# Memory-augmented recurrent transformer: another split of a PSUM copy, dense weights in more pieces, and a reordered norm in step 2

## The chip, the cores and the metric

The kernel runs on one core of one Trainium2 chip. The metric is the device time of one execution in microseconds (us). A core has five engines that run side by side: TensorE (matrix multiply, writes its results to PSUM), VectorE, ScalarE and GpSimd (elementwise work), and SyncE, which here issues the DMAs. Each engine runs its own queue of instructions in order and waits on semaphores for the others. In the profile the engines are PE (TensorE's matmuls), PEld (its weight loads), DVE (VectorE), ACT (ScalarE), POOL (GpSimd) and SP (SyncE). "L567" is line 567 of the kernel.

## The reference

Two layers, applied twice. Layer A is attention over segments of 32 tokens, with 8 memory rows that are carried from segment to segment; layer B is a two-matrix feed-forward with ReLU. In short:

```python
# x [1, 2048, 512], 64 segments of 32 tokens; 32 heads of 128; 8 memory rows
def A(x):
    mem = mem0
    for s in range(64):
        h = concat([mem, x[32*s : 32*s+32]])          # 40 rows
        q, k, v = h @ Wq, h @ Wk, h @ Wv              # 32 heads x 128
        p = softmax(mask(q @ k.T * 128**-0.5))        # 40 x 40 a head
        o = (p @ v) @ Wo                              # 40 x 512
        mem, out[s] = o[:8], o[8:]                    # memory for the next segment
def B(x): return relu(x @ w1) @ w2                    # 512 -> 1376 -> 512
x = x + A(layernorm(x)); x = x + B(layernorm(x))
x = x + A(layernorm(x)); x = x + B(layernorm(x))      # same weights
```

## The kernel before

**Steps.** The memory makes the 64 segments of a layer sequential. The kernel interleaves the two passes: step k handles segment k of the first pass (layer index 0) and segment k - 3 of the second (index 1), so that there are 67 steps, 0 to 66. Steps 0 to 2 and 64 to 66 have one pass only ("single"), steps 3 to 63 have both. The dense layer of a segment runs one step behind its attention.

**Order.** TensorE, VectorE, SyncE and GpSimd run in the order in which `step` writes their instructions (`tc.manual_schedule`); ScalarE's order is chosen by the framework's scheduler, with the blocks under `tc.high_priority` first.

**One step.** In `step(k)`:

- `qk(0, ..)` (L567) computes queries and keys of heads 0 to 15 in three batches. ScalarE copies the queries out of PSUM (L573, QT), VectorE the keys (L575, KT). `behind={n: f}` calls f after batch n.
- `load_values` and `load_memory_values` issue the DMAs that bring the values of the tokens and of the memory rows into `Vs`; `transpose_step` issues a transposing DMA that turns the normalized rows `XN` of the step before into `xnT`, input of the dense layer and of the second pass.
- `masks` (L593) writes the mask into a score bank, `scores` (L601) adds q times k to it, `exponentials` (L619 maximum, L623 subtract, L625 exponential on ScalarE) and `softmax` (L635 sum, L636 reciprocal, L639 multiply) make the probabilities.
- `probabilities` finishes the softmax of the first sixteen heads behind the first batch of the second `qk`, turns it by a transposing DMA (`turn_p`) and, in step 1, calls `load_dense`, which loads all dense weights (w1 1376 KB, w2 1280 and 96 KB). Until then w1's and w2's tiles serve as staging for values (`first_step`).
- `dense_h` (L510, hp) and `dense_y` (L526, into the second score bank sp) are the dense layer; `values1` (L373, v) makes the values of the second pass for the next step; `output_late` (wox) and `add_late` (L420) finish the second pass's output.
- `turn_second` turns the second sixteen heads' probabilities with TensorE (L655) into PSUM and copies them to `PT_sb` (L660). In steps with both passes there are four tiles: u = 0 and 1 (eight heads each), g = 0 and 1. The two of u = 0 lie in the pool `ps_c`, those of u = 1 in `ps_fill`.
- `weighted_v` (L692, pv) multiplies by the values into three tiles a pass: heads 0 to 11, 12 to 23 and 24 to 31. The second tiles take the `ps_c` banks of u = 0, the third ones the `ps_fill` banks of u = 1. `outputs` (L709) copies them to `OTm` and `OTx`.
- `output_mem` (L609, wo), `new_memory` (which starts `output_own`, L387), `make_room` (the rest of `output_own`) and `memory_values` (L767, vm) make the next memory and its values. `prepare` adds the residual and norms the step's rows (`moments` L260, `normalize_parts` L271 to L283, with GpSimd's power at L278).

**Step 2** is special: there the second pass starts. `first_later`, called behind the first `qk` batch of the second half, adds the dense layer of segment 0 (`add_dense`), norms the result for the second pass, writes it to the upper half of `XN` and turns it by DMA; `values1(3, ..)` reads the result before `dense_y`.

Of the kernel before, what the change touches and what calls it, by code (L numbers as in the profile page):

```python
# [22 lines left out]
def kernel(  # L23
# [14 lines left out]
    nc = tc.nc  # L38
    _, S, Dm = A_x.shape
# [3 lines left out]
    Dff = B_w1.shape[1]  # L43
# [26 lines left out]
    def has0(k):  # L70
        return 0 <= k < NSEG

    def has1(k):
        return DELTA <= k <= LAST
# [79 lines left out]
    w1_flat = w1_sb[:].rearrange("p c f -> p (c f)")  # L154
    w2_flat = w2_sb[:].rearrange("p c d -> p (c d)")

    def load_dense():
        nc.sync.dma_start(out=w1_sb[:], in_=B_w1.rearrange("(c p) f -> p c f", p=128))
        nc.sync.dma_start(out=w2_sb[:, 0:NFC - 1, :],
                          in_=B_w2[F_LAST:Dff, :].rearrange("(c p) d -> p c d", p=128))  # L160
        nc.sync.dma_start(out=w2_sb[0:F_LAST, NFC - 1, :], in_=B_w2[0:F_LAST, :])

    mhalf_t = const.tile([128, 2], F32)
# [94 lines left out]
    def moments(d, i):  # L258
        n = 64 if i else 64 * slots(d)
        nc.vector.bn_stats(out=stats_all[0:n, i, 0, :], in_=residual(d)[0:n, :])  # L260
# [2 lines left out]
        later = has1(k + 1) and k > 2  # L263
        return [(k - 1, 0)] + ([(k - 2, 1)] if later else [])

    def normalize_parts(parts):
        i0, i1 = parts[0][1], parts[-1][1] + 1
        for q in range(2 * max(slots(d) if i == 0 else 1 for d, i in parts)):
            o = q ^ 1
            j0, j1 = (i0, i1) if q < 2 else (0, 1)  # L270
            nc.vector.tensor_copy(out=stats_all[32 * q:32 * q + 32, j0:j1, 1, :],  # L271
                                  in_=stats_all[32 * o:32 * o + 32, j0:j1, 0, :])
        mv = wk.tile([128, 2, 3], F32, tag="ln_mv", bufs=2, name="mv")
        for _, i in parts:
            nc.vector.bn_aggr(out=mv[:, i, 0:2], in_=stats_all[:, i].rearrange("p n s -> p (n s)"))
        rstd = mv[:, i0:i1, 2]
        nc.vector.tensor_scalar_add(out=rstd, in0=mv[:, i0:i1, 1], scalar1=LN_EPS)
        nc.gpsimd.tensor_tensor(out=rstd, in0=rstd, in1=mhalf_t[:, 0:i1 - i0], op=ALU.pow)  # L278

        def rows():  # L280
            for d, i in parts:
                n = 64 if i else 64 * slots(d)
                nc.vector.tensor_scalar(out=XN[0:n, HALF * i:HALF * i + HALF], in0=residual(d)[0:n, :],  # L283
                                        scalar1=mv[0:n, i, 0:1], scalar2=mv[0:n, i, 2:3],
                                        op0=ALU.subtract, op1=ALU.mult)

        return rows
# [9 lines left out]
    def transpose_step(k):  # L297
        tag, bufs = ("R", 8) if k == 1 else ("xnT", 1)
        t = xnT_tiles[k] = wk.tile([128, NC4, 128], BF, tag=tag, bufs=bufs, name="xnT")
        n = 2 if k < 3 else NC4  # L300
        nc.sync.dma_start_transpose(out=t[:, 0:n, :], in_=XN[:, 0:128 * n])

    def first_later():

        add_dense(0)
        moments(0, 1)
        normalize_parts([(0, 1)])()
        nc.sync.dma_start_transpose(out=xnT_tiles[2][:, 2:4, :], in_=XN[:, HALF:Dm])

    def later_rows(k):  # L310
        return [xnT_tiles[k][:, 2 + c4 % 2, SEG * (c4 // 2):SEG * (c4 // 2) + SEG] for c4 in range(NC4)]
# [49 lines left out]
    def values1(s, ii, late=False):  # L361
        if not has1(s):
            return
        if ii == 0:
            vd1[s] = dram.tile([2, 4, 32, 512], BF, tag="vd1", bufs=3, name="vd1")
        values_tile(later_rows(s - 1), ii, vd1[s], late=late)
# [164 lines left out]
    def add_dense(d):  # L531
        n = 64 * slots(d)
        R = residual(d)
        if not has0(d):
            ob = obs[d] = wk.tile([128, HALF], BF, tag="ob", bufs=1, name="ob")
            nc.vector.tensor_tensor(out=ob[0:n, :], in0=R[0:n, :], in1=sp_banks[1][0:n, 0:HALF], op=ALU.add)
        else:
            nc.vector.tensor_tensor(out=R[0:n, :], in0=R[0:n, :], in1=sp_banks[1][0:n, 0:HALF], op=ALU.add)
            g, o = place1(d + DELTA)
            nc.gpsimd.tensor_copy(out=residual(g)[64 * o:64 * o + 64, :], in_=R[0:64, :])  # L540
# [40 lines left out]
    def qk(hf, act, between=None, behind=None):  # L581
        res = []
        for n, (o, nh) in enumerate(BATCHES):
            res.append((o, nh) + qk_batch(n, 16 * hf + o, nh, act[0], act[-1] + 1, None if n else between))
            if behind and n in behind:
                behind[n]()
            if hf and n > 0 and (n == 2 or len(act) == 1):
                masks(*act[n - 1:n])
        return res
# [38 lines left out]
    def softmax(hf, act, by_pe=False, ess=None):  # L628
        if ess is None:
            ess = exponentials(act)  # L630
        if by_pe and hf:
            transpose_p()
        for a, es in ess.items():
            sm = wk.tile([128, 8], F32, tag="sm", bufs=2)
            nc.vector.tensor_reduce(out=sm[:], in_=es[:], axis=AX.X, op=ALU.add)  # L635
            nc.vector.reciprocal(out=sm[:], in_=sm[:])  # L636
            eng = nc.vector if by_pe or (hf, a) == (1, act[-1]) else nc.gpsimd
            P = P1_sb if hf else P_sb
            eng.tensor_tensor(out=P[:, :, 64 * a:64 * a + L], in0=es[:],  # L639
                              in1=sm[:].unsqueeze(2).to_broadcast([128, 8, L]), op=ALU.mult)  # L640

    def turn_second(single=False):

        tps = {}
        for u in range(2):
            for g in range(2):
                if single and u:
                    tps[u, g] = tps[0, g][:, 4:8]
                    continue
                pool, tag = (ps_fill, "fill") if u else (ps_c, "c")  # L650
                tps[u, g] = pool.tile([128, 8 if single else 4, L], F32, tag=tag, name="tp")
            for sl in range(4):
                for g in range(2):
                    R = 64 * g
                    nc.tensor.matmul(tps[u, g][:, sl, :], lhsT=P1_sb[R:R + L, 4 * u + sl, :],  # L655
                                     rhs=ident[R:R + L, R:R + L], start=True, stop=True)
        ns = 8 if single else 4
        for s0 in range(0, 8, ns):
            for g, copy in ((0, nc.scalar.copy), (1, nc.vector.tensor_copy)):
                copy(out=PT_sb[:, s0:s0 + ns, g, :], in_=tps[s0 // 4, g][:, 0:ns])  # L660

    def transpose_p():
# [111 lines left out]
    def load_memory_values(k, act):  # L774
        for ii in range(2):
            for a in act:
                nc.sync.dma_start(out=Vs[64 * a:64 * a + M, 2048 * ii:2048 * (ii + 1)].rearrange("m (j e) -> m j e", j=4),
                            in_=vmds[k][ii, :, a * M:(a + 1) * M, :].rearrange("j t e -> t j e"))
# [82 lines left out]
    def make_room(k):  # L861
        if has0(k):
            output_own(k, H // 2, H)
        else:
            values1(k + 1, 1)
        output_ride(k)
# [49 lines left out]
    def step(k):  # L916
# [33 lines left out]
        value_group(k, 0, 0, 2)  # L950
        value_unit(k, 0)
        with tc.high_priority(offset=PRIO):
            transpose_step(k)
            load_memory_values(k, act)
            scores(qks, act)
            ess = exponentials(act)
            if not single:
                masks(act[0])
# [3 lines left out]
        def probabilities():  # L962

            softmax(0, act, by_pe, ess)
            if not by_pe:
                turn_p()
            if k % 4 == 3 and has_x:
                inputs_T(n_x)
            if has0(k + 1):
                load_x(k + 1)  # L970
            if k == 1:
                load_dense()

        def turn_first():
            probabilities()
            if k == 2:
                first_later()

        with tc.high_priority(offset=PRIO):
            qks = qk(1, act, behind={0: turn_first})  # L980
        if single:
            output_late(k, first, second)
        if k != LAST and not (single and has0(k)):
            dense_h(d)
        with tc.high_priority(offset=PRIO):
            scores(qks, act)
            softmax(1, act, by_pe)
        evict_behind.append(last_exp[0].ins)
        value_group(k, 0, 2, NC4, late=True)
        value_unit(k, 1)  # L990
# [4 lines left out]
        if k == LAST:  # L995
            dense_h(d, slice(0, 1))
        output_late(k, second, H)
        if has0(k) and has1(k + 1):
            values1(k + 1, 0)
        if not (single and has0(k)):  # L1000
            value_group(k, 1, late=True)
        value_group(k, 2, late=True)
        if has0(k) and has1(k + 1):
            values1(k + 1, 1, late=True)
        evict_behind.clear()
        if k == LAST:
# [9 lines left out]
            mom["x"] = stat_tail(mom["stats"])  # L1016
        with tc.high_priority(offset=PRIO):
            turn_second(single)
        tokens_in(k + 1)
        if k < LAST and spare_T(k + 1) is not None:  # L1020
            nc.gpsimd.tensor_copy(out=HTm[:, :, 2 * M:32], in_=spare_T(k + 1))
# [16 lines left out]
        if cont:  # L1038
            with tc.high_priority(offset=PRIO):
                new_memory(k, cont, wo)  # L1040
            make_room(k)
            with tc.high_priority(offset=PRIO):
                memory_values(k + 1)
        with tc.high_priority(offset=PRIO):
# [3 lines left out]
    with tc.manual_schedule(engines={mybir.EngineType.PE, mybir.EngineType.DVE, mybir.EngineType.SP,  # L1048
# [22 lines left out]
        d = LAST  # L1071
# [59 lines left out]
```

## Time and profile before

| | |
|---|---|
| time, median of 3 runs | 1604.52 us (1602.91 to 1607.10) |
| the profiled execution | 1602.26 us, span 1600.5 us |
| TensorE matmul busy | 1557.4 us (97%), 47090 matmuls |
| VectorE, ScalarE, GpSimd busy | 1257.0 (79%), 740.6 (46%), 299.2 (19%) us |
| granted TensorE clock, mean | 0.998 |
| DMA | 144.18 MB in 233452 packets, mean 90 GB/s |

Times in the profile count from the first instruction of the span. A timeline line has the start, the duration, engine, line, operation, output<-inputs, shapes and the number of merged instructions; in brackets stand the engine's idle time before it and what ended it. "Issue" is time in which an engine waited for nothing that the profile shows.

### The profile page before, as it was taken

To read this page: it belongs to the slowest core of one execution; us is meant where nothing else is said; L and a number is where in the kernel's file an instruction comes from. 1 tells how busy PE (TensorE), PEld (TensorE's weight loads), DVE (VectorE), ACT (ScalarE), POOL (GpSimd) and SP (SyncE) were. 2 spreads that over 40 slices of the span, in tenths; PEclk is the share of its full clock that TensorE was granted. 3 is DMA by queue.
4 is the path that set the end of the run, shared out by engine and by line. 5 is a ranking of instruction groups with operands and counts; after the bars stand their busy time and mean duration, and the time that the engine had idled before them with its cause. 6 is when DMAs were issued, how large, how long until landed. Compare 5 with 4: busy or idle time off the path is not lost.

```text
span 1600.5 us, 104152 instructions
## 1 busy us (share of the span) xinstructions
PE 1557.4 (97%) x47090; PEld 1300.0 (81%) x47090; DVE 1257.0 (79%) x3587; ACT 740.6 (46%) x1817; POOL 299.2 (19%) x606
## 2 busy tenths in 40 slices
PE   6999999999999999999999999999999999999998
PEld 4678888878888888887888888888888888888876
DVE  4467888888888788887887888888888888888875
ACT  3434444444454444444444444544444444444443
POOL 2011121122121112112212211211221121121110
PEclk9999999999999999999999999999999999999999
DMA  9723233333433333333433434343233334224321
GB/s 371 235 69 79 79 78 84 89 67 93 79 79 84 83 79 77 85 85 67 92 79 76 88 78 86 76 90 80 75 87 77 79 76 85 78 71 88 72 68 39
DMA packets 233452, 144.18 MB, mean 90 GB/s; under 512 B 124936, under 2 KB 229424, under 8 KB 233008
## 3 DMA queue, kind: packets, MB, share of 16 engines
q1 hardware_dynamic: 232912, 137.48, 36.1%
q8 instruction: 369, 6.05, 1.7%
q14 instruction: 75, 0.61, 0.2%
q10 hardware_dynamic: 96, 0.03, 0.0%
HBM read 65.41 MB, written 45.09 MB: 69 GB/s over the span
## 4 chain that ended last, share of the span: by engine, by line
PE 81%; DVE 7%; issue 2%; ACT 1%; DMA 1%; POOL 0%; POOLq 0%; ACTq 0%
PE qp L567 35%; PE wo L609 7%; PE vm L767 7%; PE own L387 7%; PE hp L510 5%; PE v L373 4%; PE sp L601 3%; PE pv L692 3%; PE vp L807 3%; PE sp L526 3%; PE wox L387 2%; DVE R L420 1%; DVE sm L635 1%; DVE P_sb L639 1%; DVE es L623 1%
## 5 line engine op out<-in xcount | busy, mean ns | idle before, releaser
L573 ACT CAST QT<-qp 128x480 bf16<-128x480 f32 (+3 forms) x402 | 200.5, 499 | 396.0 <-PE qp L567 394.0
L567 PE MATMUL qp<-HT,Wq_sb 128*128 128x80 bf16 (+1 forms) x8576 | 367.8, 200 | 1.9 <-POOL HT L753 1.2
L567 PEld LDWEIGHTS <-Wq_sb 128*128 128x128 bf16 x8576 | 323.3, 100 | 33.2 <-issue 27.6
L567 PE MATMUL qp<-HT,Wk_sb 128*128 128x80 bf16 (+1 forms) x8576 | 344.7, 200 | 1.7 <-ACT QT L573 0.9
L567 PEld LDWEIGHTS <-Wk_sb 128*128 128x128 bf16 x8576 | 317.3, 100 | 2.8 <-issue 2.2
L639 POOL TENSOR_TENSOR P_sb<-es,sm 128x320 bf16<-128x320 f32 x186 | 132.0, 724 | 698.8 <-ACT es L625 410.2
L575 DVE CAST KT<-qp 128x480 bf16<-128x480 f32 (+3 forms) x402 | 220.2, 573 | 27.4 <-PE qp L567 24.0
L619 DVE TENSOR_REDUCE mx<-sp 128x8 f32<-128x320 f32 x256 | 114.3, 486 | 132.3 <-PE sp L601 132.3
L387 PEld LDWEIGHTS <-OTx 128*32 128x32 bf16 x6272 | 156.9, 96 | 29.3 <-issue 12.0
L625 ACT ACTIVATE es<-es 128x320 f32<-128x320 f32 x256 | 109.3, 468 | 69.3 <-DVE es L623 69.1
L387 PE MATMUL own<-Wo_sb,OTx 128*32 128x256 bf16 x4096 | 132.8, 272 | 1.7 <-issue 1.5
L767 PE MATMUL vm<-Wv_sb,HTm 128*32 128x512 bf16 x2144 | 128.9, 379 | 0.0
L609 PE MATMUL wo<-Wo_sb,OTm 128*32 128x512 bf16 x2112 | 127.9, 380 | 0.7 <-issue 0.6
L771 ACT CAST VmS<-vm 128x512 bf16<-128x512 f32 x132 | 77.4, 586 | 105.3 <-PE vm L767 98.9
L635 DVE TENSOR_REDUCE sm<-es 128x8 f32<-128x320 f32 x256 | 117.2, 458 | 10.9 <-ACT es L625 2.1
L373 PE MATMUL v<-Wv_sb,xnT 128*32 128x512 bf16 x2048 | 123.2, 382 | 0.2 <-DMA xnT<-XN 0.2
L593 DVE CAST sp<-maskb 128x320 f32<-128x320 bf16 x256 | 118.3, 483 | 0.0
L623 DVE TENSOR_TENSOR es<-sp,mx 128x320 f32<-128x320 f32 x256 | 113.0, 480 | 0.5
L278 POOL TENSOR_TENSOR mv<-mv,mhalf_t 128x2 f32<-128x2 f32 (+1 forms) x67 | 45.7, 682 | 302.4 <-DMA vmd<-VmS 153.4
L510 PE MATMUL hp<-xnT,w_sb 128*128 128x64 bf16 (+1 forms) x2948 | 96.4, 192 | 2.3 <-issue 1.2
L526 PE MATMUL sp<-w_sb,hT 128*32 128x256 bf16 (+1 forms) x2772 | 93.8, 276 | 0.3
L510 PEld LDWEIGHTS <-w_sb 128*128 128x128 bf16 x2948 | 90.5, 98 | 4.0 <-issue 3.8
(127 smaller groups left out, 2058.2 us busy)
## 6 DMA issues: line engine op xcount, KB each, us to landing
Vs<-vd SPq DMA_DIRECT2D x96, 256.0 KB
vd<-vst SPq DMA_DIRECT2D x133, 128.0 KB
vmd<-VmS SPq DMA_DIRECT2D x132, 128.0 KB
Vs<-vmd SPq DMA_DIRECT2D x254, 32.0 KB
Vs<-vmd SPq DMA_DIRECT2D x60, 128.0 KB
vd<-vst SPq DMA_DIRECT2D x96, 64.0 KB
Wq_sb<-in_A_Wq_dram SPq DMA_DIRECT2D x2, 2048.0 KB
Wk_sb<-in_A_Wk_dram SPq DMA_DIRECT2D x2, 2048.0 KB
```

Of the source, the lines that this page charges most:

```text
L373: nc.tensor.matmul(vp[32 * j:32 * j + 32, :], lhsT=tokens[c4], rhs=Wv_sb[:, c4, n * 512:(n + 1) * 512], start=(c4 == 0), stop=(c4 == NC4 - ...
L387: nc.tensor.matmul(t[q:q + 32, 0:HALF], lhsT=OTx[:, h, SEG * a:SEG * a + SEG], rhs=Wo_sb[:, h, HALF * j:HALF * j + HALF], start=(h < h0 + ...
L510: nc.tensor.matmul(hp[:, fc - f0, 0:n].rearrange("p (s t) -> p s t", s=ns), lhsT=w1_sb[:, c4, u:u + 128], rhs=cols(c4), start=(c4 == 0), s ...
L526: nc.tensor.matmul(sp_banks[1][32 * q:32 * q + 32, 0:w], lhsT=hT_tiles[d][0:fs, fc, SEG * o:SEG * o + SEG], rhs=w2_flat[0:fs, fc * Dm + HA ...
L567: nc.tensor.matmul(qp[:, hi, 0:ncol], lhsT=W_sb[:, c4, h * Dh:(h + 1) * Dh], rhs=HT[:, c4, a_lo:a_hi, :], start=(c4 == 0), stop=(c4 == NC4 ...
L573: nc.scalar.copy(out=dst[:, 0:nh, a_lo * L:a_hi * L], in_=qp[:, 0:nh, 0:ncol])
L575: nc.vector.tensor_copy(out=dst[:, 0:nh, a_lo * L:a_hi * L], in_=qp[:, 0:nh, 0:ncol])
L609: nc.tensor.matmul(wo[32 * j:32 * j + 32, :], lhsT=OTm[:, h, n, 2 * M * c:2 * M * c + 4 * M], rhs=Wo_sb[:, h, :], start=(h < 4), stop=(h > ...
L623: nc.vector.tensor_tensor(out=es[:], in0=sp, in1=mxs[a][:].unsqueeze(2).to_broadcast([128, 8, L]), op=ALU.subtract)
L635: nc.vector.tensor_reduce(out=sm[:], in_=es[:], axis=AX.X, op=ALU.add)
L639: eng.tensor_tensor(out=P[:, :, 64 * a:64 * a + L], in0=es[:], in1=sm[:].unsqueeze(2).to_broadcast([128, 8, L]), op=ALU.mult)
L767: nc.tensor.matmul(vp[32 * j:32 * j + 32, :], lhsT=HTm[:, c4, :], rhs=Wv_sb[:, c4, n * 512:(n + 1) * 512], start=(c4 == 0), stop=(c4 == NC ...
```

## The change

It has three parts.

1. `turn_second`: in steps with both passes the first three of the four copies run on ScalarE and the last on VectorE; before, they alternated. Single steps keep one copy each.
2. Dense weights: `load_dense` (three DMAs) becomes `load_w1` (four row blocks), `load_w2` (four ranges) and `load_w2_rest`. Two blocks of w1 are issued in step 1 ahead of `load_memory_values`, and `transpose_step(1)` goes behind those; the other two and the rest of w2 stand where `load_dense` stood; the four ranges of w2 follow `turn_second` of step 1.
3. Step 2: `first_later` goes. `add_dense(0)` stays in place; the statistics (`later_spread`) go behind the second batch, the aggregate and the reciprocal root between scores and their maximum, the normalized rows and their transposing DMA between the exponential and the sums. `values1(3, ..)` moves from before `dense_y` to behind `make_room(2)`.

```diff
-    def load_dense():
-        nc.sync.dma_start(out=w1_sb[:], in_=B_w1.rearrange("(c p) f -> p c f", p=128))
-        nc.sync.dma_start(out=w2_sb[:, 0:NFC - 1, :],
-                          in_=B_w2[F_LAST:Dff, :].rearrange("(c p) d -> p c d", p=128))
+    def load_w1(*cs):
+        for c in cs:
+            nc.sync.dma_start(out=w1_sb[:, c, :], in_=B_w1[128 * c:128 * c + 128, :])
+
+    def load_w2(lo, hi):
+        nc.sync.dma_start(out=w2_sb[:, lo:hi, :],
+                          in_=B_w2[F_LAST + 128 * lo:F_LAST + 128 * hi, :].rearrange("(c p) d -> p c d", p=128))
+
+    def load_w2_rest():
         nc.sync.dma_start(out=w2_sb[0:F_LAST, NFC - 1, :], in_=B_w2[0:F_LAST, :])
...
-    def first_later():
-
-        add_dense(0)
-        moments(0, 1)
-        normalize_parts([(0, 1)])()
-        nc.sync.dma_start_transpose(out=xnT_tiles[2][:, 2:4, :], in_=XN[:, HALF:Dm])
...
         ns = 8 if single else 4
         for s0 in range(0, 8, ns):
-            for g, copy in ((0, nc.scalar.copy), (1, nc.vector.tensor_copy)):
+            for g in range(2):
+                copy = nc.vector.tensor_copy if g and s0 == 8 - ns else nc.scalar.copy
                 copy(out=PT_sb[:, s0:s0 + ns, g, :], in_=tps[s0 // 4, g][:, 0:ns])
...
         with tc.high_priority(offset=PRIO):
-            transpose_step(k)
-            load_memory_values(k, act)
+            if k == 1:
+                load_w1(0, 1)
+                load_memory_values(k, act)
+                transpose_step(k)
+            else:
+                transpose_step(k)
+                load_memory_values(k, act)
...
             if k == 1:
-                load_dense()
-
-        def turn_first():
-            probabilities()
+                load_w1(2, 3)
+                load_w2_rest()
             if k == 2:
-                first_later()
+                add_dense(0)
+
+        def later_spread():
+            if k == 2:
+                moments(0, 1)
+                spread([(0, 1)])
 
         with tc.high_priority(offset=PRIO):
-            qks = qk(1, act, behind={0: turn_first})
+            qks = qk(1, act, behind={0: probabilities, 1: later_spread})
...
             scores(qks, act)
-            softmax(1, act, by_pe)
+            rows = normalize_parts([(0, 1)], False) if k == 2 else None
+            ess = exponentials(act)
+            if rows:
+                rows()
+                nc.sync.dma_start_transpose(out=xnT_tiles[2][:, 2:4, :], in_=XN[:, HALF:Dm])
+            softmax(1, act, by_pe, ess)
...
-        if has0(k) and has1(k + 1):
+        if k > 2 and has0(k) and has1(k + 1):
             values1(k + 1, 0)
...
-        if has0(k) and has1(k + 1):
+        if k > 2 and has0(k) and has1(k + 1):
             values1(k + 1, 1, late=True)
...
             turn_second(single)
+        if k == 1:
+            for lo, hi in ((0, 3), (3, 6), (6, 8), (8, 10)):
+                load_w2(lo, hi)
...
             make_room(k)
+            if k == 2:
+                for ii in range(2):
+                    values1(k + 1, ii)
             with tc.high_priority(offset=PRIO):
                 memory_values(k + 1)
```

`spread` holds the two or more small copies that `normalize_parts` made first; `normalize_parts(parts, False)` leaves them out.

More of the change, by code (lines that the diff above doesn't have):

```diff
@@ L264, in norm_parts, with spread @@
         return [(k - 1, 0)] + ([(k - 2, 1)] if later else [])
-    def normalize_parts(parts):
+    def spread(parts):
         i0, i1 = parts[0][1], parts[-1][1] + 1
@@ L272, in normalize_parts @@
                                   in_=stats_all[32 * o:32 * o + 32, j0:j1, 0, :])
+    def normalize_parts(parts, spreads=True):
+        i0, i1 = parts[0][1], parts[-1][1] + 1
+        if spreads:
+            spread(parts)
         mv = wk.tile([128, 2, 3], F32, tag="ln_mv", bufs=2, name="mv")
```

## Prediction

> **What bounds the kernel now.** I read the page first, for which engine sets the end.
>
> ```profile
> PE 1557.4 (97%) x47090; PEld 1300.0 (81%) x47090; DVE 1257.0 (79%) x3587; ACT 740.6 (46%) x1817; POOL 299.2 (19%) x606
> PE 81%; DVE 7%; issue 2%; ACT 1%; DMA 1%; POOL 0%; POOLq 0%; ACTq 0%
> ```
>
> TensorE is busy for 97% of the span (1600.5 us) and holds 81% of the chain that ended last. The change removes no matmul, so it can only win or lose in TensorE's idle time and in stretches where its clock is low. The table of TensorE's waits says where that is:
>
> ```profile
> PE pv L692 <- DVE PT_sb L660: 8.0, 29, 0.6
> PE sp L601 <- DVE sp L593: 2.9, 2, 2.5
> PE hp L510 <- issue: 1.2, 1, 1.2
> PE qp L567 <- ACT QT L573: 0.9, 1, 0.9
> ```
>
> Columns: sum, times, longest. The first row recurs through the kernel; the other three are nearly all step 2, which lasts 29.8 us (72.1 to 101.9) where step 3 lasts 22.5 with more matmuls. The timeline of TensorE in step 2:
>
> ```profile
> 73.78 0.77 PE L567 MATMUL qp<-HT,Wk_sb 128*128 128x40 bf16 x24 [0.89 <-ACT QT L573]
> ...
> 78.33 0.67 PE L510 MATMUL hp<-xnT,w_sb 128*128 128x32 bf16 x20 [1.19 <-issue]
> ...
> 79.67 2.58 PE L526 MATMUL sp<-w_sb,hT 128*32 128x320 bf16 x22
> ...
> 88.30 0.45 PE L601 MATMUL sp<-KT,QT 128*40 128x40 bf16 x16 [2.52 <-DVE sp L593]
> ...
> 90.62 3.24 PE L373 MATMUL v<-Wv_sb,xnT 128*32 128x512 bf16 x32 [0.20 <-DMA xnT<-XN]
> 93.69 1.39 PE L526 MATMUL sp<-w_sb,hT 128*32 128x320 bf16 x22
> ```
>
> The same 22 dense matmuls take 2.58 us at 79.67 and 1.39 at 93.69, and values1's 32 take 3.24 where step 3's take 1.91. The table by stretches says why (PEclk is the granted clock):
>
> ```profile
> core 0: us, PE busy (x) PEld busy (x) DVE busy (x) ACT busy (x) POOL busy (x), PEclk, DMA share, GB/s
> ...
> 79.60:82.20 2.60, 2.60 (x35) 1.60 (x28) 0.98 (x2) 0.47 (x1) 0.00 (x0) 0.52 0.07 17
> ...
> 90.60:93.70 3.10, 3.08 (x34) 1.19 (x36) 1.86 (x6) 1.05 (x3) 1.02 (x4) 0.55 0.14 48
> ```
>
> So each group of gaps in step 2 is followed by about 3.4 us at half clock.
>
> **Part 1, turned probabilities.** Steps 3 to 63 turn the second half's probabilities into four PSUM banks; pv's second tile reuses the banks of the first two copies. Two kinds of step, on time (the first two lines) and late:
>
> ```profile
> 187.92 0.49 ACT L660 CAST PT_sb<-tp 128x160 bf16<-128x160 f32 x2 [0.82 <-PE tp L655]
> 187.96 0.56 DVE L660 CAST PT_sb<-tp 128x160 bf16<-128x160 f32 x2
> ...
> 258.23 0.56 DVE L660 CAST PT_sb<-tp 128x160 bf16<-128x160 f32 x2
> 258.61 0.25 PE L692 MATMUL pv<-PT,Vs 40*128 40x40 bf16 x7 [0.18 <-DVE PT_sb L660]
> ```
>
> Times from the first transposing matmul: ScalarE's copies end at 0.594 and 0.788, in every step. VectorE's first ends at 0.66 on time; late, behind add_late and the input's statistics, it ends at 0.88 to 1.40. pv's 26th matmul starts 0.052 after that copy's end (0.714 on time), and wo 0.587 after that matmul; from there TensorE runs without a gap. In the new order ScalarE's second copy is the one pv waits for: it ends at 0.788, so that matmul starts at 0.840. On time that costs 0.840 - 0.714 = 0.127; I count 33 such steps: +4.2. Late steps gain: eight start at about 1.00 (-0.16), eleven at 1.066 (-0.225), one at 0.933 (-0.09), and eight at 1.17 or 1.45. Those eight gain only 0.304, because VectorE's one remaining copy, which the third tile needs at 0.840 + 24 x 0.0127 = 1.144, is late next. Sum -6.3; net **-2.1**. ScalarE's third copy (to 0.98) pushes its OTm copies by about 0.1; wo needs the first at 1.427 and has it by 1.11. Bounds: if three copies in a row don't overlap (0.297 apart, not 0.19), pv starts at 0.943 and the net is +3.7; the other end is -2.5, since nothing later in a 23.3 us step absorbs the 0.127. I take -2.1: the row shows two in a row at 0.19.
>
> **Part 2, step 2's second norm.** VectorE before the late scores:
>
> ```profile
> 85.62 0.34 DVE L271 COPY stats_all<-stats_all 32x6 f32<-32x6 f32 x2
> 85.99 0.21 DVE L275 BATCH_NORM_AGGREGATE mv<-stats_all 128x2 f32<-128x12 f32 x1
> 86.24 0.15 DVE L277 TENSOR_SCALAR mv<-mv 128x1 f32<-128x1 f32 x1
> 87.12 0.40 DVE L283 TENSOR_SCALAR XN<-R,mv 64x256 bf16<-64x256 f32 x1 [0.73 <-POOL mv L278]
> 87.45 0.39 DVE L575 CAST KT<-qp 128x240 bf16<-128x240 f32 x1
> 87.77 0.48 DVE L593 CAST sp<-maskb 128x320 f32<-128x320 bf16 x1
> ```
>
> From the copies' end (85.96) to KT's start (87.45), 1.49 us leave the path: aggregate, add, GpSimd's power, the row. The mask ends at 86.76 and scores start there: **-1.5**; about 1.1 of the gap stays. Aggregate and add (0.36) then lie where VectorE waits for scores, and the row (0.40) where it waits for ScalarE's exponential (0.54 idle at 90.34). Its transposing DMA is behind turn_p's on SP as before; GpSimd's copy into HT and values1 read it, the latter now some 8 us later.
>
> values1(3) leaves this place. Scores to tp took 6.72 (88.30 to 95.02). Without it: scores 0.27, vp 0.55, hp 1.30, about 0.65 of uncovered wait for the relu of hp, dense_y 1.33: 4.1, **-2.6**. The softmax (about 3.4 behind scores) fits. It returns before memory_values(3) for 1.90 at full clock, and its second tile takes own's buffer, which VectorE frees 1.1 after own ends, while the first tile covers 0.9: **+2.1**. Its store and Vs load stand ahead of vmd's, whose readers wait longer. Part 2 is **-2.0**. Bounds: -2.7 if the relu is covered; -0.3 if what idle time is left still halves the clock (dense_y 1.19 longer, about 0.5 in pv and wo).
>
> **Part 3, dense weights.** Three loads become nine; same bytes. SP now issues two w1 pieces at 58.7, where the table by stretches gives a DMA share of only 0.13 from 61 to 65, so the saturated stretch (65 to 77.5, share 0.91 to 0.98) should end near 74. Why that matters: the instruction queue moves 6.05 MB in 369 packets, 16,384 bytes each, 64 per TensorE instruction and so TensorE's program. Two of these ended at 72.41 and 76.99, and TensorE resumed after 1.37 and 1.34, at 73.78 and 78.33: both gaps are late program, started some 5 us after the request as I place it, against 1.8 at rest. The first request (about 66.4) still meets a full queue: bounds -1.04 to 0, I take 0, its own row being the nearest. The second (70.5) should be served by 75.5, before TensorE runs out at 77.0: **-1.3** (bounds -1.3 to 0). Without that gap the half clock at 79.7 goes: dense_y 2.58 to 1.39 and qp 0.98 to 0.77, **-1.4** (to 0).
> [...]
> Moved on SP: step 1's transpose slips behind the loads of memory values, from 58.7 to about 62.5; its reader is hp at 76.4. SP waits for vmd's landing until 61.8 as now. Those loads queue behind 0.7 MB; they moved at 62.5 to 63.7, and pv needs them at 65.4: about 1 us of cover, 0 to +0.6, I take 0. The w2 pieces stand behind the vd stores, ahead of vmd at 72.04.
>
> **Sum.** -2.1 - 2.0 - 1.3 - 1.4 = -6.8. The profiled run took 1602.26 (span 1600.5 and 1.76 around it): 1595.5. It is 2.26 under the median of the runs shown; I carry the difference over: 1604.52 - 6.8 = **1597.7**.
>
> **Rivals.**
> Rival 1, fetches stay late: DMA is as full at 70 to 75 as now, gap and half clock remain. For it: the bytes are the same and the first late fetch is in no term. Against: 0.7 MB goes out before 65. -4.1: 1600.4. Chance 0.25.
> Rival 2, the gaps left in the late half of step 2 (1.1 and 0.65 us, 2 us apart, among short matmuls) again halve the clock: 1597.7 + 1.7 = 1599.4. For it: 1.2 us sufficed at 77. Against: about 1.8 us idle where there were 2.7. Chance 0.15.
> Rival 3, slower: every piece holds SP as the worst issue does. The 96-row piece of w2 at 65.22 held it for 2.45 us. Nine such issues and 5.2 us of others from 58.7 put the last w2 piece at 86, landing near 88; dense_y, at 79.7, waits 8.4, pv in step 1 about 0.9, and half clock follows (1.7): -4.1 + 11.0 = +6.9, 1611.4. It decides once the mean hold passes 1.3 us (last landing after 77.3). Against: issues of 128 rows took 0.33 to 0.46. Chance 0.08.
> [...]
> That ScalarE's copies don't overlap (+3.7 in part 1, 1603.5) has 0.04.
>
> **How the numbers follow.** The forecast has 0.46, 0.02 is for the unforeseen. A measurement of this kernel can tell about 0.3%, 4.8 us: below 1599.7 is faster. The forecast, most of rival 2 and a little of rival 1 lie there: 0.60. Rival 3 and the unforeseen: slower 0.10. The rest is 0.30. Range: down to 1593.5 (first fetch, relu and 2 us of the runs' own scatter), up to 1605 (rivals 1 and 2 together are 1602.1, with scatter); it leaves out rival 3.
>
> **What would show it.** Steps 3 to 63 all near 23.42 us, none at 23.6 or at 23.29, and the row of pv behind VectorE's PT_sb nearly gone; 183 copies by ScalarE. Step 2 near 24 us: scores behind the mask about 1.1, no gap in hp, dense_y at 1.4. Wrong if steps are longer than 23.5, if clock 0.5 still stands in step 2, or if pv in step 1 waits for Vs.

## The result

The changed kernel takes 1599.88 us (median of 10 runs, 1597.17 to 1602.18), the kernel before 1604.76 beside it: ratio 0.9970, 95% interval 0.9958 to 0.9982. That is 4.9 us less, where 6.8 were predicted (interval 2.9 to 6.7 us). The profiled execution of the changed kernel took 1600.23 us, span 1598.5.

The page of the changed kernel, its busy times and its chain:

```profile
PE 1562.6 (98%) x47089; PEld 1302.2 (81%) x47090; DVE 1245.6 (78%) x3526; ACT 745.8 (47%) x1878; POOL 299.8 (19%) x606
PE 87%; DVE 1%; DMA 1%; issue 1%; POOL 0%; ACT 0%; POOLq 0%; ACTq 0%
```

VectorE's share of the chain fell from 7% to 1%, TensorE's rose by 6 points: most waits for VectorE are gone. TensorE's busy time grew by 5.2 us, although the change adds no matmul, so part of the idle time that went came back as matmuls that take longer. TensorE's waits:

```profile
PE pv L696 <- DMA Vs<-vmd: 1.7, 1, 1.7
PE sp L604 <- DVE sp L596: 1.6, 3, 0.8
...
PE pv L696 <- DVE PT_sb L664: 0.6, 3, 0.2
```

The wait for VectorE's copies of turned probabilities went from 8.0 us (29 times) to 0.6. The first row is new: in step 1 pv waits for the memory values. The timeline of TensorE there:

```profile
67.68 0.57 PE L696 MATMUL pv<-PT,Vs 40*128 40x40 bf16 x16 [1.74 <-DMA Vs<-vmd]
68.09 0.56 PE L696 MATMUL pv<-PT_sb,Vs 40*128 40x40 bf16 x16
68.58 2.85 PE L612 MATMUL wo<-Wo_sb,OTm 128*32 128x512 bf16 x32
71.20 1.83 PE L390 MATMUL own<-Wo_sb,OTx 128*32 128x256 bf16 x32
```

Before, the same wo took 1.91 and the same own 1.05, with no wait ahead of them. Step 1 grew from 21.28 to 24.41 us. Step 2 fell from 29.78 to 24.27:

```profile
76.29 0.75 PE L570 MATMUL qp<-HT,Wk_sb 128*128 128x40 bf16 x24
...
78.89 1.40 PE L513 MATMUL hp<-xnT,w_sb 128*128 128x32 bf16 x44
...
80.97 1.41 PE L529 MATMUL sp<-w_sb,hT 128*32 128x320 bf16 x22
...
86.74 0.58 PE L604 MATMUL sp<-KT,QT 128*40 128x40 bf16 x16 [0.85 <-DVE sp L596]
...
89.70 1.41 PE L529 MATMUL sp<-w_sb,hT 128*32 128x320 bf16 x22 [0.73 <-ACT hT L519]
91.03 0.37 PE L658 MATMUL tp<-ident,P_sb 40*128 40x40 bf16 x16
...
96.09 2.20 PE L376 MATMUL v<-Wv_sb,xnT 128*32 128x512 bf16 x32
```

The gaps at qp and hp are gone, the gap ahead of the scores is 0.85 instead of 2.52, both dense outputs take 1.41. The table by stretches shows where the half clock is now:

```profile
core 0: us, PE busy (x) PEld busy (x) DVE busy (x) ACT busy (x) POOL busy (x), PEclk, DMA share, GB/s
69.40:72.80 3.40, 3.40 (x55) 1.98 (x48) 0.31 (x1) 0.59 (x1) 0.00 (x0) 0.50 0.89 292
79.60:82.20 2.60, 2.60 (x64) 2.08 (x62) 0.98 (x2) 0.48 (x3) 0.00 (x0) 1.00 0.67 186
...
90.60:93.70 3.10, 2.89 (x82) 2.00 (x80) 2.25 (x9) 1.05 (x3) 1.26 (x4) 1.00 0.15 44
```

Two slices of 3.41 us at a clock of 0.50 have left step 2 (at 79.71 and 89.95 before), one has come to step 1 (at 69.39). Between the two profiled executions: step 3 begins 1.96 us earlier (99.94 instead of 101.90), steps 3 to 63 take 1.45 less (1431.07 instead of 1432.52), and what comes from step 64 on takes 1.3 more.

### The profile page after: what moved, and what is told of

Same layout as the page of the kernel before. It is cut to its first block, busy times and chain, and to the rows that moved or that the text cites. A ratio compares the mean times of both kernels' runs of the same rounds, so it can differ in the third digit from the quotient of the medians.

```text
span 1598.5 us, 104157 instructions
## 1 busy us (share of the span) xinstructions
PE 1562.6 (98%) x47089; PEld 1302.2 (81%) x47090; DVE 1245.6 (78%) x3526; ACT 745.8 (47%) x1878; POOL 299.8 (19%) x606
## 4 chain that ended last, share of the span: by engine, by line
PE 87%; DVE 1%; DMA 1%; issue 1%; POOL 0%; ACT 0%; POOLq 0%; ACTq 0%
PE qp L570 35%; PE wo L612 7%; PE vm L771 7%; PE own L390 7%; PE v L376 6%; PE hp L513 5%; PE sp L529 4%; PE pv L696 4%; PE wox L390 4%; PE sp L604 3%; PE vp L811 3%; PE tp L658 1%; DMA xnT<-XN 1%; PE sp L696 0%; PE mt L835 0%
## 5 line engine op out<-in xcount | busy, mean ns | idle before, releaser
L771 PEld LDWEIGHTS <-HTm 128*32 128x32 bf16 x2144 | 59.8, 97 | 41.3 <-issue 2.3
```

The lines of the kernel that those rows point to most:

```text
L771: nc.tensor.matmul(vp[32 * j:32 * j + 32, :], lhsT=HTm[:, c4, :], rhs=Wv_sb[:, c4, n * 512:(n + 1) * 512], start=(c4 == 0), stop=(c4 == NC ...
```

## Experiments

Theory: the terms of the prediction hold each by itself, except that the two pieces of w1 ahead of the memory values cost step 1 what they save in step 2. Rivals: the copies bring more than their own sum, or the loads bring nothing. Each ratio is to the kernel before on the same chip. The experiments ran on other chips than the comparison above; the kernel before took 1599.6 to 1600.4 us there in median, so only ratios are set side by side. 0.001 is 1.6 us.

**One part at a time.** Part 1 alone:

```diff
-            for g, copy in ((0, nc.scalar.copy), (1, nc.vector.tensor_copy)):
+            for g in range(2):
+                copy = nc.vector.tensor_copy if g and s0 == 8 - ns else nc.scalar.copy
```

> The kernel before with part 1 alone (three of four copies on ScalarE). Theory: in steps 3 to 63 pv's 26th matmul starts 0.84 us after the first transposing matmul and wo at 1.43 in every step, so on-time steps lose 0.13 and late ones gain 0.09 to 0.30: -2.1 us in all, near 1602.7 against 1604.8 (ratio 0.9987); steps 1 and 2 stay as before (21.3 and 29.8 us, the gaps at qp, hp and the mask in place). Rival: the whole gain of the change (-4.9) is in these 61 steps, and step 2 paid for itself: then -4 to -5 here. Rival: late steps gain nothing because VectorE's remaining copy is late too: +4.

Ratio 0.9971 (0.9961 to 0.9980): 4.6 us less (3.2 to 6.2). That is the first rival's figure; the 2.1 of the theory lies outside the interval. Part 2 alone:

```diff
-            qks = qk(1, act, behind={0: turn_first})
+            qks = qk(1, act, behind={0: probabilities, 1: later_spread})
...
+            rows = normalize_parts([(0, 1)], False) if k == 2 else None
...
-        if has0(k) and has1(k + 1):
+        if k > 2 and has0(k) and has1(k + 1):
...
+                for ii in range(2):
+                    values1(k + 1, ii)
```

> The kernel before with part 2 alone (step 2's second norm and values1(3) moved). Theory: the scores behind the mask wait about 0.9 to 1.1 us instead of 2.5, dense_y waits 0.7 for the relu, values1 takes twice 1.0 instead of 3.2, and the second half-clock stretch (at 90) is gone; the gaps at qp and hp and the first half-clock stretch stay, since the loads are as before: step 2 near 27.8 instead of 29.8, total -2.0 (ratio 0.9988). Rival: what gaps remain halve the clock again: half clock at about 90 stays and step 2 is 29 or more, total 0 to -0.5.

Ratio 0.9992 (0.9981 to 1.0004): 1.3 us less, from 3.0 less to 0.6 more. TensorE's timeline in step 2, and a stretch of the table:

```profile
89.47 2.59 PE L524 MATMUL sp<-w_sb,hT 128*32 128x320 bf16 x22 [0.72 <-ACT hT L514]
...
93.70 3.60 PE L607 MATMUL wo<-Wo_sb,OTm 128*32 128x512 bf16 x32
```

```profile
88.80:99.00 10.20, 9.41 (x154) 5.80 (x158) 4.01 (x12) 2.25 (x6) 1.66 (x5) 0.50 0.09 23
```

The gaps that are left (1.07 ahead of the scores, 0.72 ahead of dense_y) were followed by half clock for 10.2 us (0.50 in the table), three times 3.41: the prediction's rival 2, at its dearest. But this is one execution, the slowest of the twelve (1601.62 us at a mean granted clock of 0.996); the other eleven had 0.997 to 1.000. Part 3 alone:

```diff
-                load_dense()
+                load_w1(2, 3)
+                load_w2_rest()
...
+                load_w1(0, 1)
+                load_memory_values(k, act)
+                transpose_step(k)
...
+            for lo, hi in ((0, 3), (3, 6), (6, 8), (8, 10)):
+                load_w2(lo, hi)
```

> The kernel before with part 3 alone (nine loads instead of three, two w1 blocks ahead of the memory values' loads). Theory: TensorE's program arrives in time, so the gaps at qp and hp in step 2 (0.9 and 1.2 us) and the half clock behind them go: step 2 shorter by 3 to 3.8, to about 26; but pv in step 1 waits 1.7 us for the memory values and half clock follows: step 1 longer by about 3.1, to 24.4. Sum -0.5 (ratio 0.9997). Rival: step 2's early gaps belong to ScalarE's copy of QT and not to the loads: they stay, and the total is +3.

Ratio 1.0003 (0.9992 to 1.0014): 0.5 us more, from 1.3 less to 2.2 more. The gap at qp is gone, but hp's is 1.73. Step 1 takes 21.41 us (24.4 expected) and step 2 28.94 (26 expected): the theory's total was met, but not in the way that it gave. The three parts by themselves make 4.6 + 1.3 - 0.5 = 5.4 us, the change as a whole 4.9.

**The order of the first two pieces.**

```diff
-                load_w1(0, 1)
                 load_memory_values(k, act)
+                load_w1(0, 1)
                 transpose_step(k)
```

> The changed kernel with one swap in step 1: load_memory_values is issued before load_w1(0, 1) instead of behind it. Theory (the memory values queued behind 0.7 MB of w1): pv in step 1 no longer waits (1.7 us now), the half clock in wo and own goes, step 1 is 21.3 instead of 24.4, and step 2 stays at 24.3: -3.1 against the changed kernel, near 1596.8 or 0.995 of before. Rival: w1 is issued some 2.5 us later, since SyncE first waits for the memory values to land in DRAM, so the transfers crowd into 66 to 76 again and step 2's early gaps and half clock return: 3 to 4 us come back and the total stays near 1600.

Ratio 0.9971 (0.9959 to 0.9984), as the changed kernel: the rival's result. TensorE's timeline:

```profile
75.37 0.75 PE L513 MATMUL hp<-xnT,w_sb 128*128 128x32 bf16 x24
78.81 0.67 PE L513 MATMUL hp<-xnT,w_sb 128*128 128x32 bf16 x20 [2.69 <-issue]
...
80.15 2.20 PE L529 MATMUL sp<-w_sb,hT 128*32 128x320 bf16 x22
```

Step 1 is 21.22 us again, without the wait, and arrives at hp 3.5 us earlier than in the changed kernel; there TensorE stands still for 2.69 and goes on at 78.81. What step 1 had lost, step 2 loses now.

```diff
             if k == 1:
+                load_w1(0, 1)
                 memory_values(k)
...
-                load_w1(0, 1)
                 load_memory_values(k, act)
```

> The changed kernel with the first two pieces of the dense weights issued ahead of step 1's memory values' writes, where SP's queue stands idle for about 3 us, instead of between those writes and the loads behind them. Theory (what step 1 lost is only the order: 0.70 MB between the write and the load): step 1's wait of TensorE for the memory values (1.74 us) and the half clock behind it go, step 1 is near 21.3 us instead of 24.4, while step 2 stays near 24.3 us, since the bytes are as early as in the changed kernel; about 3 us under the changed kernel, ratio to the kernel before about 0.995. Rival (the bytes moved one after the other: whatever the order, a program fetch or a load comes late by about as much): a gap of 1 to 2.7 us ahead of step 2's first dense matmuls or in step 1, and ratio 0.997.

Ratio 0.9979 (0.9969 to 0.9988): the rival's result. The wait in step 1 is 0.65, but a half clock follows it (67.74 to 71.16), and hp has a gap of 0.80 and goes on at 79.24.

```diff
-                load_w1(0, 1)
+                load_w1(0, 1, 2, 3)
                 load_memory_values(k, act)
...
-                load_w1(2, 3)
                 load_w2_rest()
```

> The changed kernel with all four pieces of the first dense weights ahead of the loads of step 1's memory values, 1.41 MB instead of 0.70 MB. Theory (the loads land behind the bytes that are queued before them): another 0.70 MB at the 313 GB/s of this stage is 2.25 us more of TensorE's wait, 4.0 us instead of 1.74, and step 1 near 26.7 us. Rival (only the issues ahead of them count, 0.45 us each): the wait grows by 0.9 us, to 2.6, and step 1 is near 25.3 us.

Ratio 0.9974 (0.9964 to 0.9984). SP's queue and TensorE's timeline:

```profile
58.88 2.83 SPq L159 DMA_DIRECT2D w_sb<-in_B_w_dram  x4
62.61 0.70 SPq L781 DMA_DIRECT2D Vs<-vmd  x2
```

```profile
68.46 0.56 PE L696 MATMUL pv<-PT,Vs 40*128 40x40 bf16 x16 [2.29 <-DMA Vs<-vmd]
...
69.47 3.57 PE L612 MATMUL wo<-Wo_sb,OTm 128*32 128x512 bf16 x32
```

The wait is 2.29, below both figures (4.0 by the bytes, at the 313 GB/s that the kernel before moved from 69.4 to 77.5; 2.6 by the issues): neither account is complete. Step 1 takes 25.65 us, and still the kernel is no slower than the others.

**Does the gap halve the clock?** Seven matmuls that nobody reads fill the wait:

```diff
         with tc.high_priority(offset=PRIO):
+            if k == 1:
+                keep_busy(7)
             pvs = weighted_v(act)
```

> The changed kernel with seven idle 128x512 matmuls ahead of step 1's sums of values, whose results nobody reads; at 0.22 to 0.24 us each they fill 1.6 us of the wait of 1.74 us. The memory values come no earlier. Theory (the wait costs twice: by itself, and by a half clock of 3.4 us that an idle TensorE brings on): no slice of step 1 at half clock, its output product takes 1.91 us and not 2.85, its own output 1.05 and not 1.84, and step 1 about 23.0 us instead of 24.4. Rival (the half clock comes from the stage and not from the gap): the output product stays at 2.85 us and step 1 at 24.4 us or more.

Ratio 0.9957 (0.9943 to 0.9972). TensorE's timeline and the stretch that was at half clock:

```profile
65.69 1.68 PE L918 MATMUL idle<-Wo_sb,ident 128*128 128x512 bf16 x7
67.30 0.56 PE L696 MATMUL pv<-PT,Vs 40*128 40x40 bf16 x16
...
68.20 1.91 PE L612 MATMUL wo<-Wo_sb,OTm 128*32 128x512 bf16 x32
69.94 1.05 PE L390 MATMUL own<-Wo_sb,OTx 128*32 128x256 bf16 x32
```

```profile
69.40:72.80 3.40, 3.40 (x116) 2.45 (x108) 1.00 (x4) 0.58 (x1) 0.00 (x0) 1.00 0.95 292
```

Clock 1.00, wo 1.91, own 1.05: with the idle time filled, no half clock follows here, nor in the last experiment, which fills the gap too. Step 1 is 22.57 us (23.0 expected).

**The two terms of part 1.** In the changed kernel, ScalarE takes the extra copy only in late steps:

```diff
+        late = len(units_at(k)) < 2 or (k % 4 == 1 and k // 4 + 4 < NXT)
...
-                copy = nc.vector.tensor_copy if g and s0 == 8 - ns else nc.scalar.copy
+                copy = nc.vector.tensor_copy if g and (s0 == 8 - ns or not late) else nc.scalar.copy
```

> The changed kernel, but ScalarE takes the extra copy of turned probabilities only in the 28 steps whose turned probabilities land late; in the 33 on-time steps VectorE copies two banks, as before. Theory (the two terms of the prediction's part 1 are both real, and the rest of the difference between runs is late program): the 33 on-time steps fall from 23.42 or 23.46 us back to 23.29 or 23.33, which is 33 x 0.127 = 4.2 us less than the changed kernel; the late ones stay as in the changed kernel. With the changed kernel 4.9 us under the kernel before, this comes to about 9 us under it, ratio 0.9944. Rival (ScalarE's copies help everywhere, since the copies alone gave 4.5 us and not 2.1): the on-time steps gain nothing or lose, and the ratio stays at 0.997 or above.

Ratio 0.9950 (0.9935 to 0.9965): 8.0 us less (5.6 to 10.4). The same on the kernel before, without parts 2 and 3:

```diff
-            for g, copy in ((0, nc.scalar.copy), (1, nc.vector.tensor_copy)):
+            for g in range(2):
+                copy = nc.vector.tensor_copy if g and (s0 == 8 - ns or not late) else nc.scalar.copy
```

> The kernel before, with ScalarE taking the extra copy of turned probabilities only in steps 1 and 2 and in the 28 late steps of steps 3 to 63; loads and second norm as before. Theory (the late term of the prediction's part 1): 6.3 us less in those 28 steps, ratio 0.9961; steps such as 4, 8 and 15 fall by 0.2 to 0.3 us, the others stay at 23.29 or 23.33. Rival (the copies alone gained 4.5 us where the terms make 2.1, so the late term is the larger part: 8.7): ratio 0.9946.

Ratio 0.9965 (0.9952 to 0.9978): 5.6 us less (3.5 to 7.7), which holds the theory's 6.3 and leaves out the rival's 8.7. And with only the on-time steps changed:

```diff
+                copy = nc.vector.tensor_copy if g and (s0 == 8 - ns or late) else nc.scalar.copy
```

> The kernel before, with ScalarE taking the extra copy only in the 33 steps where no turned probabilities were late. Theory (the on-time term of part 1): 33 x 0.127 = 4.2 us more, ratio 1.0026; the steps at 23.29 and 23.33 go to 23.42 and 23.46. Rival (the copies alone gained 4.5 and not 2.1 because the on-time steps cost less than 0.127 each when their sum is measured, 1.8 us in all): ratio 1.0011.

Ratio 1.0017 (1.0007 to 1.0027): 2.7 us more (1.1 to 4.3), which holds both figures. The kernel before once more, unchanged:

> The kernel before, unchanged, profiled on this chip, to set steps 3 to 63 beside those of the experiments. Theory (the steps are the same on any chip, and what differs between profiled executions is late program): the shortest steps are 23.29 and 23.33 again, and steps 3 to 63 take between 1428.5 and 1432.5 us, as in the two experiments without the copies. Rival (the copies also take late program away): near 1430 here and never under 1428, while kernels with the copies stay under 1426.5.

1601.51 us; steps 3 to 63 take 1430.41, shortest steps 23.29 and 23.33, as the theory said. The rival's 1428 is not undercut either, so this run does not part the two. The changed kernel has the copies and does not stay under the rival's 1426.5 (1431.07), but its relatives do, and whether the copies also take late program away stays open. Last, adaptive copies and filled gap together, the changed kernel with both edits:

```diff
+                copy = nc.vector.tensor_copy if g and (s0 == 8 - ns or not late) else nc.scalar.copy
...
+            if k == 1:
+                keep_busy(7)
```

> The changed kernel with both edits that gained: the extra copy on ScalarE in late steps only, and seven idle matmuls ahead of step 1's sums of values. Theory (the terms add, since they lie in other steps): the filled gap measured 6.9 us under the kernel before, and the 33 on-time steps give 4.2 us more, 11.1 in all, ratio 0.9931. Rival (in the start the gain of one is taken back by the next late program, so that a step 1 without the wait is followed by a longer step 2): no better than the adaptive copies alone, ratio 0.995.

Ratio 0.9960 (0.9943 to 0.9976): 6.4 us less, near the rival's figure; the 11.1 of the theory lies outside the interval. Steps 3 to 63 are the shortest of all (1423.7), but the filler adds nothing that the whole time shows. The seven executions of this one kernel differ in the clock: two at a mean granted clock of 1.000 took 1588.5 and 1590.6 us (the second is the profiled one), two at 0.996 took 1596.9 and 1597.9. So a profile without half clock does not say that the kernel is free of it.

The adaptive version has the lowest ratio, 8.0 us under the kernel before. Its interval (0.9935 to 0.9965) overlaps those of the changed kernel (0.9958 to 0.9982), of the filled gap and of the late copies, so the whole times do not decide which is best. The steps show what the edit is worth: the 33 on-time steps take 772.1 us, where the six kernels with copies everywhere take 774.0 to 775.9.

## Why the prediction was right, and where it was not

The forecast, faster by a few us, came true, and 4.9 us is just over the 4.8 that it called measurable. Of its three causes two hold, and the third brought nothing. Its working can be held against 14 profiled executions.

**Part 1** holds in sign and mechanism. ScalarE takes the three copies in a row, in step 7 of the changed kernel:

```profile
186.02 0.68 ACT L664 CAST PT_sb<-tp 128x160 bf16<-128x160 f32 x3 [0.82 <-PE tp L658]
```

They end 0.595, 0.789 and 0.985 us after the first transposing matmul, and pv's 26th matmul starts at 0.840: the numbers of the prediction. Steps 3 to 63, split as predicted into 33 on-time and 28 late steps (the range of the executions, us; step 3, which is on time, has ScalarE's extra copy in "late steps only" too):

| kernels | on time | late |
|---|---|---|
| copies as before (4 executions) | 771.4 to 774.2 | 656.9 to 658.5 |
| three on ScalarE (5; the changed kernel apart) | 774.0 to 775.4 | 650.5 to 651.4 |
| the changed kernel | 775.9 | 655.2 |
| late steps only (3) | 772.1 to 772.5 | 651.2 to 652.6 |
| on-time steps only (1) | 775.8 | 657.8 |

Over all 14 executions, by the medians of each step with the extra copy and without it, the late term is -6.1 (predicted -6.3) and the on-time term +2.9 (predicted +4.2): net -3.2 and not -2.1, at the edge of the interval of part 1 alone. Taking the shortest of each step over its executions, the terms are -6.7 and +4.2; that a step which is late for another reason hides part of its 0.127 would explain the lower on-time median, but this is argued. The 4.6 that part 1 alone brought is more than either sum, and why stays open.

The changed kernel's own profiled execution lost 3.8 to 4.7 us in the late steps against its five relatives. TensorE's idle time in steps 3 to 63 is 13.39 us before and 6.63 there (4.23 to 4.99 in the relatives), yet these steps took only 1.45 less: the rest is matmuls that follow each other more slowly, in steps that differ from run to run. So the -1.45 us between the two profiles understates this part. The relatives lie 6.3 to 7.9 under the same execution of the kernel before; but that execution is the longest of the four with the old copies (1428.5 to 1432.5 for steps 3 to 63), and against the shortest they lie 2.3 to 4.0 under it. One sign that the prediction set against itself, steps longer than 23.5 us, came: 22 of the 61 steps are longer in the changed kernel, 26 before, 6 to 14 in the relatives.

**Part 2** holds term by term in the profiles; in the whole time its 1.3 us (3.0 less to 0.6 more) could be nothing. The table's columns run between these moments: hp resumes (after its gap, or starts, if it has none), late scores, turning matmuls, step 3. A star marks a stretch in which a slice of 3.41 us at half clock lies:

| kernel | step 2 begins | hp's gap | hp resumes | to scores | to turning | to step 3 |
|---|---|---|---|---|---|---|
| before | 72.13 | 1.19 | 78.33 | 9.97* | 6.72* | 6.88 |
| before again (e11) | 72.72 | 0.91 | 79.18 | 8.56 | 6.13* | 6.88 |
| copies (e1) | 72.33 | 0.92 | 78.17 | 8.56 | 6.36* | 6.89 |
| late copies (e9) | 72.24 | 1.18 | 79.09 | 8.56 | 6.25* | 6.88 |
| on-time copies (e10) | 72.37 | 0.92 | 78.31 | 8.56 | 6.30* | 6.88 |
| norm (e2) | 72.94 | 0.91 | 79.41 | 7.12 | 5.47* | 11.70* |
| loads (e3) | 72.30 | 1.73 | 78.06 | 10.08* | 6.22* | 6.88 |
| the change | 75.67 | 0 | 78.89 | 7.86 | 4.29 | 8.91 |
| w1 behind (e4) | 72.16 | 2.69 | 78.81 | 8.32* | 4.29 | 8.91 |
| adaptive (e5) | 72.54 | 1.78 | 78.29 | 8.50* | 5.47* | 8.99 |
| w1 early (e6) | 74.47 | 0.80 | 79.24 | 7.11 | 4.29 | 8.91 |
| gap filled (e7) | 73.66 | 0.45 | 77.90 | 7.29 | 4.29 | 8.91 |
| all w1 ahead (e8) | 76.61 | 0 | 79.82 | 7.71 | 5.47* | 8.99 |
| adaptive, filled (e12) | 73.57 | 1.05 | 78.41 | 7.29 | 4.29 | 8.91 |

(The change and e8 do all 44 matmuls of hp behind the moment in column 4, the others 20 to 27, so their fifth column is up to 0.6 longer.) To the scores: 8.56 becomes 7.12, -1.44 (predicted -1.5). Scores to turning: 6.72 becomes 4.29, -2.43 (predicted -2.6). Behind it: 6.88 becomes 8.91, +2.03 (predicted +2.1). Rival 2 was probably underrated: of the eight profiled executions with the new norm it struck three (the 5.47s, 1.18 us, and in e2 2.8 more behind it), where the prediction gave it 0.15. One execution of each kernel is a small sample; the idle time ahead of half clock in them stands in the last section. With the old norm a slice lies behind the gap of 2.52 in all six. (The 6.72 is itself the longest of those: against the others, 6.13 to 6.36, the step gains 1.8 to 2.1.)

**Part 3** is the part of the working that failed, in two steps, and the changed kernel's own profile hides it. The prediction took 0 for the first late fetch, -1.3 for the second and -1.4 for the half clock behind it. The half clock was priced right (9.97 or 10.08 to the scores against 8.56, 1.4 to 1.5), but which fetch the loads bring in time was not. The first gap is gone in all eight kernels with the new loads, and is 0.79 to 1.53 in the six without. The second stays in six of eight, up to 2.69. The column "hp resumes" says why: 77.90 to 79.82, with whatever loads, and however early step 2 began. In the twelve executions with that gap TensorE resumed 1.27 to 1.57 us after a 16,384-byte program packet ended; that this packet holds what hp waits for is concluded from this steady distance, as no record names its contents. The new loads move the fetch ahead of it (that one ends at 70.8 to 72.7 instead of 72.4 to 73.8; in e8 it ends at 74.2, well before step 2 begins) but not this one, which starts at 75.6 to 76.9 instead of 75.8 to 77.1 (77.7 in e8). The saturated stretch did not end near 74: the DMA share of the changed kernel from 74 to 76 us is 1.06. So a step 1 that ends earlier only waits longer at hp, and one that ends later, as in the changed kernel and in e8, finds its program there. The changed kernel loses the gap because it comes 3.5 us late. No record shows when a packet is asked for: the prediction's requests at 66.4 and 70.5 and its 1.8 us at rest are its author's estimate, and the records give the packets' own starts and ends alone.

The step "about 1 us of cover, 0 to +0.6, I take 0" was the second to fail: 1.74 us, and a half clock behind it that costs 0.94 in wo and 0.78 in own. It was named as what would prove the prediction wrong (pv in step 1 waits for Vs). It cost the whole little, since hp goes on at 77.9 to 79.8 in any case. The size of the wait differs with the same order: 1.74 in the changed kernel, 0.38 in e3, 0.40 in e5. SP's queue of the changed kernel and that of e5:

```profile
61.67 0.93 SPq L159 DMA_DIRECT2D w_sb<-in_B_w_dram  x2
63.04 0.69 SPq L781 DMA_DIRECT2D Vs<-vmd  x2
```

```profile
60.80 0.92 SPq L159 DMA_DIRECT2D w_sb<-in_B_w_dram  x2
62.44 0.69 SPq L782 DMA_DIRECT2D Vs<-vmd  x2
```

The issues are 0.6 to 0.9 us apart, the landings 2.0: the packet records show w1's last packet ending at 66.90 and 64.29, the memory values' at 67.21 and 65.20. In the changed kernel a program packet (64.50 to 65.59) ran while w1's packets were still moving (62.77 to 66.90), in e5 (64.17 to 65.30) when nearly all were through. Whether the one held up the other the records do not show.

Rival 1 (fetches stay late) is thus the truer account of the loads: alone they brought nothing (+0.5, -1.3 to +2.2). Rival 3 is refuted: in the changed kernel the issues of pieces took 0.38 to 0.59 us, one 1.11, and that of the 96 rows 0.43 instead of 2.45. The overlap of ScalarE's copies was right. That the total came near is luck in part: by themselves the copies brought 4.6 us (2.1 predicted), the norm 1.3 (2.0) and the loads -0.5 (2.7), and these errors cancel.

The twelve gaps at hp, late program if the conclusion above holds, are of 0.45 to 2.69 us, behind stretches with a DMA share near 1 (1.06 from 74 to 76 us in e7).

## What to carry to other kernels

Work out a moved copy per step class: one edit had a term of -6.1 us in steps where the old engine was late and +2.9 where it was not, and alone in the first class it brought 5.6 us, alone in the second it cost 2.7. Time won or lost ahead of hp moved it little here (77.90 to 79.82 us, with step 2 beginning anywhere from 72.13 to 76.61), so look for a moment that stays put over several variants before pricing a gap. Price idle time of TensorE by its sum over a stretch, as the next section has it, and not by the longest gap: half clock followed a longest gap of 0.65 us in e6 and not the one of 0.89 at qp in the kernel before. And compare several executions before naming a difference of 5 us in 1600: one profiled execution of the change gave 1.45 us in steps 3 to 63 where its relatives gave 6.3 to 7.9.

## What the runs showed of the hardware

No gap in step 1 of e6 was longer than 0.65 us (1.17 us idle in all from 63 to 68), and half clock followed (0.50 from 68 to 70); gaps of about 1.06 and 0.73 us in step 2 (0.85 ahead of the scores in the changed kernel) were followed by it in three profiled executions and not in five. Half clock came in slices of 3.413 us, at 79.71 and 89.95 in the kernel before and at 69.39 in the changed kernel; the clock records of both end in a shorter one (0.51 and 1.97 us). In e2 it lasted 10.2 us (0.50 from 88.8 to 99.0), the length of three. In the kernel before the second slice starts 3 times 3.413 us behind the first, and the last one 446 times.

If the executions are cut into stretches of 3.413 us at the start of a slice, half clock went with the sum of TensorE's idle time in the stretch ahead of it and not with the longest gap. Between 30 and 1570 us that sum is 1.18 and 1.76 us ahead of the two slices of the kernel before and at most 0.88 in its other stretches; in the changed kernel it is 1.69 ahead of the slice and at most 1.04 elsewhere. Over all 14, the eleven stretches with 1.62 us idle or more were all followed by a slice, five of the eight with 1.13 to 1.53 were, and of those with less only two were, which lay in half clock already (e2). The gaps of e6's step 1 add up to 1.17 us in one stretch. The two gaps of step 2 put 1.13 to 1.22 us into one stretch in the three executions with half clock, and at most 1.10 in the other five.

The 16,384-byte program packets took 0.9 to 2.3 us each between 60 and 86 us: 0.91 to 1.24 in the kernel before, 0.96 to 1.79 in the changed kernel.
